# Holding each load back until the third last one has landed, in a fused SSM-convolution and MLP kernel

## The chip, the cores and the metric

The kernel runs on one core of a Trainium2 chip. The core has a tensor engine (PE, with its weight loads shown apart as PEld), a vector engine (DVE), a scalar engine (ACT), GpSimd (POOL) and a sync engine (SP) that issues most transfers. The transfers themselves are carried by 16 DMA engines. The metric is the device time of one execution in microseconds; lower is better.

## The reference

A block of sequence length S = 2048 and width D = 640. First a long convolution with a gate (H3 style), then an MLP with the Mish activation, both with a LayerNorm ahead and a residual sum behind:

```python
x = A_q
h = x + A_ref(layernorm(x), A_k, A_v, A_shift_k, A_ssm_k, A_ssm_D)
h2 = h + B_ref(layernorm(h), B_w1, B_b1, B_w2)

def A_ref(q, k, v, shift_k, ssm_k, ssm_D):
    k_shift = sum over t of k[s - 3 + t] * shift_k[:, 3 - t]     # 4 taps along the sequence
    kv = k_shift * v
    y = irfft(rfft(kv, 2S) * rfft(ssm_k, 2S))[:S]                # causal convolution, per channel
    return q * (y + kv * ssm_D)

def B_ref(x, w1, b1, w2):                                         # F = 1728
    a = x @ w1 + b1
    return (a * tanh(softplus(a))) @ w2
```

The sum over t is written here in short; the reference pads and adds four shifted copies. All inputs and the output are bf16.

## The kernel before

The convolution is done as a transform in matrix products. Stage s1 multiplies by a 128-point table (`cst`), stage s2 by a twiddle table G (128 matrices of 128 x 128), for the filter `ssm_k` (names s1k, s2k) and for the data kv (s1v, s2v). The two spectra are multiplied on DVE and POOL (p1, p2, with pair-swapped copies made by transfers, sw), and stages i1 and i2 go back. The MLP follows in five units of 256 or 512 rows: m1 (x @ w1), Mish on ACT (hb), m2 (@ w2), residual on DVE, output.

What the program does is cut into about a thousand named steps. A step is an object with a function that emits its instructions. The list `ORDER` (lines 26 to 96) gives every step with its engine (t = PE, a = ACT, v = DVE, p = POOL, d = a transfer issued by SP, s = one issued by ACT). `_schedule` (line 175) walks that list, gives each step an estimated start and assigns buffers in turn; the steps are then sorted by that start (line 932) and emitted one after the other (lines 933 to 938). Each engine carries out its own instructions in the order of emission. The framework adds the semaphore waits that data dependencies need; transfers take eight semaphores in turn, and a transfer waits until the earlier holder of its semaphore has landed.

The loads from HBM at the head of the kernel, all issued by SP:

- d_n0 to d_n4 (line 523), 512 KB each: the filter, into `rn`. Steps k1pe transpose it on PE (line 625) and k1ev copies it out of PSUM, shuffled (lines 419 and 421), into five places `kk_s`; two of these places lie over the loads n0 and n1 in `rn`.
- d_k0 to d_k3 (line 510), 640 KB each: k, into `ra`; transposed by ktpe (line 571). kv is later written over them in `ra` (line 600).
- d_v0, d_v1 (line 520), 1280 KB each: v, into `rb`, used when kv is formed (line 600). d_v0 also waits for PE, since its place holds a shuffled filter before.
- d_g0 to d_g7 (line 526), 512 KB each: table G, used by s2 (line 652 for the filter, 685 for the data).
- d_x0 (line 754), 640 KB: the first quarter of q, into `x0`, read first by the LayerNorm statistics on DVE (lines 776 and 777).

ACT issues three small transfers at the start (`cst`, `sk_r`, and the row `A_ssm_D`). In time the 20 loads come out of the sort in the order n2, n0, n3, n1, n4, k3, k2, x0, k1, g4, k0, g5, v1, g6, g0, g7, g1, v0, g3, g2.

Line 168 holds the planner's picture of PE's program being loaded in blocks while it runs: the first point at PE instruction 204, then one every 253, with two assumed durations:

```python
_MARK, _BLOCK, _FETCH, _SLOW = 204, 253, 2.2, 6.6
```

## Time and profile before

| | us |
|---|---|
| median of three runs (223.5 to 224.49) | 224.07 |
| the profiled execution | 224.86 |
| its span, from the first to the last instruction | 223.1 |
| first 5.7 us: PE busy 4.18, DMA at 217 GB/s | 5.70 |
| 43.7 to 90 us (products of the spectra, way back): PE busy 44.66 | 46.30 |
| 90 to 223 us (the MLP): PE busy 129.82, DMA at 36 GB/s | 133.00 |

The granted clock of TensorE is 1.0 throughout. The page divides the span into 40 slices of 5.6 us; one digit is the busy share in tenths:

```profile
PE   7998899999999999999999999999999999999994
...
DVE  0699989999999998999788898974400000004023
ACT  2689989999999999888870446800053454330000
POOL 1271950005596007235767714320000000000000
PEclk9999999999999999999999999999999999999999
DMA  6999991075999999100001401043350000000024
```

The first seven digits of the DMA row are the loads named above; the next block (slices 9 to 16) is the pair-swapped copies and the MLP's weights; what comes after is transposes and output. PE stands at 9 nearly throughout, but its matmuls are pipelined, and in the first 45 us it works hand in hand with DVE and ACT, which empty PSUM.

### The profile page before, as it was taken

The page shows a single profiled execution, that of the slowest core. Times are in us where ns is not written, and L with a number is a line of the kernel's source. Part 1 is how long each engine was busy: PE and PEld are TensorE (multiplying, and loading weights), DVE is VectorE, ACT ScalarE, POOL GpSimd, SP SyncE. Part 2 cuts the span into 40 slices and gives each one's busy share as a digit, 9 for nine tenths or more (in the row PEclk, how much of TensorE's full clock was granted, in tenths as well). Part 3 has the DMA queues.
Part 4 walks back from the last instruction along what each step waited for, and adds up shares of the span by engine and source line. Part 5 has one row for each costly group of instructions (what it writes and reads, how often), then busy time and mean ns, then how long its engine had stood idle before and what let it go on. Part 6 is the DMA issues. An engine that isn't in the chain of part 4 may idle for free.

```text
span 223.1 us, 6218 instructions
## 1 busy us (share of the span) xinstructions
PE 214.7 (96%) x2598; PEld 162.1 (73%) x2598; DVE 146.2 (66%) x317; ACT 134.4 (60%) x268; POOL 65.7 (29%) x106
## 2 busy tenths in 40 slices
PE   7998899999999999999999999999999999999994
PEld 2988899999877999988887644576645445675773
DVE  0699989999999998999788898974400000004023
ACT  2689989999999999888870446800053454330000
POOL 1271950005596007235767714320000000000000
PEclk9999999999999999999999999999999999999999
DMA  6999991075999999100001401043350000000024
GB/s 214 388 408 424 408 413 69 3 203 193 277 290 283 319 351 347 62 3 0 3 0 32 88 0 31 0 91 60 88 179 0 1 0 3 0 0 0 32 82 153
DMA packets 27342, 30.68 MB, mean 138 GB/s; under 512 B 9393, under 2 KB 23730, under 8 KB 26930
## 3 DMA queue, kind: packets, MB, share of 16 engines
q1 hardware_dynamic: 26880, 30.10, 41.1%
q8 instruction: 20, 0.33, 0.6%
q10 hardware_dynamic: 338, 0.18, 0.3%
q14 instruction: 8, 0.07, 0.1%
q0 software_dynamic: 96, 0.00, 0.0%
HBM read 20.45 MB, written 2.62 MB: 103 GB/s over the span
## 4 chain that ended last, share of the span: by engine, by line
PE 64%; DVE 13%; DMA 7%; ACT 7%; POOL 5%; issue 2%; SPq 0%; DVEq 0%; ACTq 0%; POOLq 0%
PE ps L915 21%; PE ps L898 19%; ACT uv L419 6%; DMA x<-in_A_q_dram 5%; PE ps L743 4%; PE ps L744 4%; PE ps L652 3%; PE ps L543 2%; PE ps L571 2%; DMA rn<-in_A_ssm_k_dram 2%; DVE st L776 2%; DVE st L822 2%; PE ps L595 2%; POOL r L782 2%; PE ps L916 2%
## 5 line engine op out<-in xcount | busy, mean ns | idle before, releaser
L915 PE MATMUL ps<-rn,uv 128*128 128x320 bf16 (+2 forms) x416 | 61.1, 299 | 0.2 <-DVE x L921 0.2
L903 ACT ACTIVATE uv<-ps,b1s 128x512 bf16<-128x512 f32 (+1 forms) x65 | 35.4, 610 | 39.1 <-PE ps L898 38.5
L898 PE MATMUL ps<-G 128*128 128x512 bf16 (+1 forms) x325 | 58.6, 337 | 0.0
L915 PEld LDWEIGHTS <-uv 128*128 128x128 bf16 x416 | 40.2, 98 | 17.5 <-issue 0.4
L419 ACT CAST uk<-ps 128x512 bf16<-128x512 f32 (+1 forms) x96 | 48.7, 702 | 2.6 <-PE ps L544 1.6
L898 PEld LDWEIGHTS <-G 128*128 128x128 bf16 x325 | 31.2, 98 | 23.9 <-issue 1.1
L921 DVE TENSOR_TENSOR xb<-ps,xb 128x320 bf16<-128x320 f32 (+2 forms) x12 | 5.7, 487 | 36.3 <-PE ps L916 35.8
L419 ACT CAST uv<-ps 128x512 bf16<-128x512 f32 (+2 forms) x57 | 28.7, 845 | 0.0
L921 DVE TENSOR_TENSOR xa<-ps,xa 128x320 bf16<-128x320 f32 x12 | 5.9, 488 | 21.6 <-PE ps L916 21.6
L827 POOL TENSOR_TENSOR r<-ve,mhalf 128x1 f32<-128x1 f32 x16 | 10.0, 630 | 32.7 <-DVE ve L824 32.7
L743 PE MATMUL ps<-a,uv 128*128 128x128 bf16 x160 | 18.8, 219 | 0.2
L421 DVE CAST uk<-ps 128x512 bf16<-128x512 f32 (+1 forms) x27 | 17.2, 669 | 1.4 <-PE ps L744 0.9
L743 PEld LDWEIGHTS <-uv 128*128 128x128 bf16 x160 | 17.9, 113 | 0.0
L421 DVE CAST uv<-ps 128x512 bf16<-128x512 f32 (+1 forms) x25 | 15.3, 677 | 0.0
L685 PE MATMUL ps<-uv,G 128*128 128x64 bf16 (+1 forms) x256 | 12.8, 197 | 0.8
L685 PEld LDWEIGHTS <-G 128*128 128x128 bf16 x256 | 11.1, 96 | 3.1 <-issue 2.1
L600 DVE TENSOR_TENSOR ra<-ps,rb 128x512 bf16<-128x512 f32 x20 | 12.5, 684 | 0.3 <-PE ps L596 0.3
L419 ACT CAST rb<-ps 128x512 bf16<-128x512 f32 (+1 forms) x28 | 10.6, 495 | 2.7 <-PE ps L803 2.7
L652 PE MATMUL ps<-uk,G 128*128 128x160 bf16 x128 | 12.1, 230 | 0.0
L782 POOL TENSOR_TENSOR r<-ve,mhalf 128x1 f32<-128x1 f32 x16 | 10.8, 672 | 1.3
L706 DVE TENSOR_TENSOR uv<-uv,uk 128x2048 bf16<-128x2048 bf16 (+1 forms) x11 | 10.9, 1022 | 0.0
L544 PE MATMUL ps<-cst,ra 128*64 128x128 bf16 x160 | 10.6, 220 | 0.1
(116 smaller groups left out, 376.7 us busy)
## 6 DMA issues: line engine op xcount, KB each, us to landing
G<-tab_g SPq DMA_DIRECT2D x8, 512.0 KB, 12.9
rn<-in_A_ssm_k_dram SPq DMA_DIRECT2D x5, 512.0 KB, 6.2
ra<-in_A_k_dram SPq DMA_DIRECT2D x4, 640.0 KB, 9.9
rb<-in_A_v_dram SPq DMA_DIRECT2D x2, 1280.0 KB, 13.1
G<-in_B_w_dram SPq DMA_DIRECT2D x5, 432.0 KB, 6.4
rn<-in_B_w_dram SPq DMA_DIRECT2D x1, 2080.0 KB, 9.8
rn<-uk SPq DMA_DIRECT2D x4, 512.0 KB, 5.1
rb<-uk SPq DMA_DIRECT2D x8, 256.0 KB, 7.9
```

The costliest lines, as they stand in the source:

```text
L419: nc.scalar.copy(o, i)
L421: nc.vector.tensor_copy(o, i)
L600: nc.vector.tensor_tensor(kv_w[:, m, :, 8 * h:8 * h + 8, l0:l0 + n], ps.rearrange("p (l t d) -> p d t l", l=n, t=8), raw_v[:, 8 * h:8 * h ...
L652: nc.tensor.matmul(ps[:, o:o + 160], g_v[:, f, :], KA[:, :, f, :], start=True, stop=True)
L685: nc.tensor.matmul(ps[:, fl * n:fl * n + n], g_v[:, f0 + h * kf + fl, :], VX[x][:, :, f0 + h * kf + fl, :], start=True, stop=True)
L706: eng.tensor_tensor(v, v, K[c.i][:, :, f0:f1, :], ALU.mult)
L743: nc.tensor.matmul(pz[:, k, :], V[c.i][:, dg // 4, :, dg % 4], a12[:, 0, :], start=True, stop=False)
L782: nc.gpsimd.tensor_tensor(r1[:, t2:t2 + 1], ve1[:, t2:t2 + 1], mhalf[:, 0:1], ALU.pow)
L898: nc.tensor.matmul(ph[:, 0:w], w1[:, dc, fc * P:fc * P + P], lnhT_of(u)[:, dc, 0:w], start=(dc == 0), stop=(dc == NDC - 1))
L903: nc.scalar.activation(hb_of(u)[:, fc, 0:w], rt.tile[:, 0:w], ACT.Mish, bias=b1s[:, fc:fc + 1], scale=1.0)
L915: nc.tensor.matmul(po[:, 0:d1 - d0], hb_of(u)[:, fc, tl * P:(tl + 1) * P], w2[:, fc, d0:d1], start=(fc == 0), stop=False)
L921: nc.vector.tensor_tensor(x, rt.tile[:, 0:d1 - d0], x, ALU.add)
```

## The change

A tile `step` of one partition and 32 elements is added. Of the loads, those whose names match `d_n`, `d_k`, `d_v`, `d_g` and `d_x0` are listed in the order of emission. Ahead of each of them from the fourth on, SP issues a transfer of one element, from the first element of the load three places earlier to an own element of `step`. That transfer waits for the earlier load to have landed, and SP, which works in order, issues nothing behind it until then. These are 17 transfers. The loads, their order among each other, and every step on the other engines stay.

```diff
+    step = cpool.tile([1, 32], BF16, name="step")
...
     order.sort(key=lambda o: (o.start, seq[id(o)]))
+
+    ends = {"d_n": lambda b: raw_n[b][0:1, 0:1], "d_k": lambda h: raw_k[0:1, 4 * h * D:4 * h * D + 1], "d_v": lambda h: rb[0:1, h * half:h * half + 1],
+            "d_g": lambda i: gt[0:1, 2048 * i:2048 * i + 1], "d_x": lambda h: (x0, xa, xb)[h][0:1, 0:1]}
+    loads = [o for o in order if o.eng == "dma" and re.match(r"d_([nkvg]\d|x0)$", o.name)]
+    after = {loads[i].name: loads[i - 3].name for i in range(3, len(loads))}
     with tc.manual_schedule():
         for o in order:
+            if o.name in after:
+                i = [l.name for l in loads].index(o.name)
+                w = after[o.name]
+                nc.sync.dma_start(step[0:1, i:i + 1], ends[w[:3]](int(w[3:])))
```

## The prediction

> **What bounds the kernel now.** I read the page first, then busy time by stage, the chain of waits, and the queue of SP, where the change sits.

> ```profile
> span 223.1 us, 6218 instructions
> ...
> PE 214.7 (96%) x2598; PEld 162.1 (73%) x2598; DVE 146.2 (66%) x317; ACT 134.4 (60%) x268; POOL 65.7 (29%) x106
> ```
> ```profile
> 5.70:17.20 11.50, 10.99 (x245) 10.41 (x247) 9.07 (x18) 8.71 (x14) 5.85 (x6) 1.00 1.01 400
> 17.20:27.80 10.60, 9.20 (x233) 8.70 (x227) 10.45 (x22) 10.15 (x21) 6.52 (x8) 1.00 1.02 414
> 27.80:43.70 15.90, 15.90 (x281) 15.64 (x283) 15.13 (x27) 15.09 (x33) 3.37 (x7) 1.00 0.43 173
> ```

> Columns of the stages: length, busy us of PE, PEld, DVE, ACT and POOL with counts, granted clock, share of the DMA engines, GB/s. The change touches the first 43.7 us alone. There the transfers run at 400 to 414 GB/s until all loads are in, while PE, DVE and ACT are nearly full too, at full clock. After 43.7 us nothing in the program is different, so a shift arises before that or not at all.

> ```profile
> 0.72 4.94 DMA rn<-in_A_ssm_k_dram
> 5.68 0.34 SPq L510
> 6.06 11.13 DMA x<-in_A_q_dram
> 17.22 0.90 DVE st L776 x2
> ...
> 24.55 2.38 PE ps L571 x36
> 26.93 0.83 issue
> 27.77 0.47 PE ps L571 x4
> ```
> ```profile
> 17.22 0.89 DVE L776 BATCH_NORM_STATS2 st<-x 128x6 f32<-128x320 bf16 x2 [0.64 <-DMA x<-in_A_q_dram]
> ```

> These are the chain that ended last (start, us, what) and one row of DVE's timeline. Two places count: DVE stands 0.64 us until load d_x0 lands, and PE stands 0.83 us at 26.93 us with nothing to wait for but its own instructions.

> ```profile
> 0.72 3.50 SPq L523 DMA_DIRECT2D rn<-in_A_ssm_k_dram  x5
> 4.26 1.75 SPq L510 DMA_DIRECT2D ra<-in_A_k_dram  x2
> 6.06 0.47 SPq L754 DMA_DIRECT2D x<-in_A_q_dram  x1
> ...
> 10.84 0.33 SPq L520 DMA_DIRECT2D rb<-in_A_v_dram  x1
> ```
> ```profile
> xb<-in_A_q_dram SPq DMA_DIRECT2D x1, 960.0 KB, 5.0
> ```

> SP issues five loads back to back and has ten out by 7.1 us. It already waits: eight semaphores are shared in turn, so a load goes out once the transfer eight before it has landed. The landing records of the trace give the last arrival of each load: n2 5.67, n0 6.92, n3 8.29, n1 9.58, n4 10.83, k3 12.68, k2 15.61, x0 17.19, k1 18.77, g4 20.05, k0 21.63, g5 22.89, v1 26.01, g6 27.28, g0 28.55, g7 29.81, g1 31.08, v0 34.28, g3 35.44, g2 36.68. They arrive in order, 1.25 us apart for 512 KB, 1.57 for 640 KB, 3.1 for 1280 KB. Each load is spread over 16 engines; the fastest finish 1.4 us (n2) to 2.7 us (v0) before the last.

> First uses, from the instructions that wait on these semaphores, give the slack: x0 0.0 (used at 17.22), n1 0.3 (9.89), n4 0.6 (11.40), k2 0.6 (16.22); every load from k1 on 2.6 us (g0, used at 31.16) or more (v1 3.0, k0 3.4, g7 3.6, v0 3.7, g3 3.7).

> **The change, part by part.** (1) 17 one-element copies are added on SP, one ahead of each load from the fourth on. The nearest issue rows take 0.33 us (L520 above), so 17 x 0.33 = 5.6 us of SP. SP's next work after the loads is at 43.70, and the last load would go out near 31.5: hidden. Queued behind a waiting copy are only later loads. PE, DVE, ACT and POOL keep their instructions and order.

> (2) The loads start later. A load is issued 0.02 us (seen wake, k0's issue at 8.31 after n3's landing at 8.29) + 0.33 us after the third last has landed. What it then needs beyond its bytes: d_x2 into xb, issued into an idle queue at 50.40, took 5.0 us for 960 KB, of which 960/512 x 1.25 = 2.34 are bytes, so 2.67 are fixed. So landing(i) = the later of landing(i-1) + its bytes and landing(i-3) + 0.35 + 2.67 + its bytes. Three 512 KB loads take 4.27 us instead of 3.75; for 640 KB the two loads still in flight (3.14 us) cover the 3.02. In numbers: n1 5.67 + 3.02 + 1.25 = 9.94 (+0.36), n4 11.19 (+0.36), k3 12.88 (+0.20), k2 14.53, and with the 1.35 us by which it came late before (15.61 - 12.68 - 1.57, while a piece of program was loaded on one engine) 15.88 (+0.27), x0 17.45 (+0.26). On the path: x0 +0.26 us, n1 0.05 past its slack. The later loads slip by at most 0.9 (g7 30.67, g2 37.5), inside 2.6.
> Bounds: below, 0, since the last engine never runs dry if the 0.97 us from issue to first packet (51.37 - 50.40) is all that counts: the new load is ready 0.35 + 0.97 = 1.32 us after the landing, and that engine still holds two loads, 2.5 us, less the 0.36 from its last packet to the landing (n0: 6.56 to 6.92). A gain is possible too: if another engine trails, x0 is earlier, worth at most DVE's 0.64. Above: n2 took 4.94 us for 512 KB, 3.67 fixed. Then n1 lands 10.94, n4 12.19, k2 16.53, x0 18.10 (+0.9), or 19.45 (+2.3) with the 1.35 on top. I take +0.3, nearest d_x2, an ordinary load with no small ones beside it.
> [...] This trace has 2.67, for a load from HBM issued by SP.

> (3) New holds. The copies read rn where ACT (L419, 10.15) and DVE (L421, 13.49) later overwrite loads n0 and n1 with shuffled filters, and in the built kernel these two wait for the copies. Nearest row: the 1.2 KB load of A_ssm_D on ACT's queue, on one engine beside the first loads, issued 1.61, landed 4.76: 3.15 us. Copy of n0: 6.94 + 3.15 = 10.09, just before 10.15; copy of n1: 9.60 + 3.15 = 12.75, before 13.49. Taken 0; above, the b1b loads of POOL took 5.3 to 5.6 us: 12.5 against 10.15 is 2.4, less the 0.5 us that ACT idles before 12.16, +1.9. A gain is excluded.

> (4) Instruction loading. The packet records show PE's program coming in 16 KB pieces on queue q8, on one engine each. Counted with the kernel's own 204 + 253n (line 168), PE passes the points at 10.51, 15.85, 21.74, 27.78, 35.05, 42.75, and pieces start 2.27, 3.42, 3.43, 3.67, then 0.36 and 0.53 us later: late while loads run, prompt when they don't. The third ends at 26.20, PE goes on at 27.77: the 0.83 us of "issue". With three loads in flight a piece waits for less: at 21.74 a fast engine would hold v1 until about 24.5, 2.8 us instead of 3.4, leaving 0.2 of the 0.83; the last engine holds 3.9, no gain. Ends 0 and -0.83 (a loss is excluded: fewer transfers stand ahead); I take -0.35.

> Sum: +0.3 + 0 - 0.35 = 0 (-0.05). The profiled execution took 224.86, 1.76 of it outside the span; it is 0.8 above the median 224.07, to which I apply the sum: 224.0. 0.5% (1.1 us) is about what a measurement of this kernel can tell from no change.

> **Rivals.**
> A, forecast (0.42): landings and instruction loading shift by less than 1.1 us together. For it: arrivals stay paced by the last engine, and 16 of 20 loads have slack of 0.6 us or more. 224.0, own range 223.0 to 225.1.
> B (0.25), slower: the queue runs dry. Mechanism: the loads' fixed time under load is that of n2 (3.67), not of d_x2; x0 lands +0.9 to +2.3, DVE and the chain follow one to one. It decides from a fixed time of about 3.5. For it: first packets take 0.3 to 1.4 us against 0.29 later in d_x2's own records. Against: n2 had three small loads of ACT beside it. 225.6.
> C (0.11), slower: the holds of (3); it decides once a copy takes over 3.2 us to land, by up to +1.9. For it: a copy stands behind two loads on its engine. Against: both writers come late. 225.4.
> D (0.22), faster: instruction loading turns prompt: -0.83, and x0 lands earlier, up to -0.64: -1.47, 222.6. For it: PE's wait on the chain, and the fetch at 52.01, which started 2.75 us later, when the single d_x2 was nearly through: it seems to wait for what is queued. Against: v1 stands there at just that point.
> [...]
> That the change does not hold the loads is excluded: the copies stand ahead of the loads in SP's own order.

> **How the numbers follow.** Faster by over 0.5% is D, 0.22; slower is B and C, 0.36; A is 0.42. The range has to reach both sides: 222.5 (D with 0.1 to spare) to 226.0 (B short of its +2.3), leaving out 0.1 each side at most.

> **What would show it.** SP's timeline with one load at a time from 5.7 us on, d_x0 issued near 11.2 instead of 6.06; landings within 0.5 us of those above (A), or x0 past 18 and GB/s below 370 between 5.7 and 27.8 (B); ACT L419 rn or DVE L421 rn waiting on DMA (C); the "issue" at 26.93 gone and pieces starting within 1 us (D). The forecast is wrong if the span up to 43.7 us changes by more than 1.1 us, or if anything after it does.

## The result, and the profile after

| | before | after |
|---|---|---|
| median, us | 224.18 | 232.01 (230.86 to 233.99) |
| ratio | | 1.0363, 95% interval 1.0284 to 1.0442 |
| profiled execution / its span, us | 224.86 / 223.1 | 232.57 / 230.8 |
| SP's first pair-swap transfer is issued at, us | 43.70 | 50.88 |

The kernel is slower by 7.8 us, outside the range. Of the 7.7 us by which the span grew, 7.2 have arisen when SP issues its first pair-swap transfer, which waits for the filter's spectrum; what follows adds 0.5. So the loss lies in the stage of the loads. One execution of c_free below (228.82 us) and two of cols6 (229.08 and 230.09) were longer than the others of the same kernel at a lower granted clock (0.992, 0.992 and 0.993 against 0.998 or more); the ratios leave these out, the medians count them.

Top of the page of the kernel after:

```profile
span 230.8 us, 6247 instructions
...
PE 217.8 (94%) x2598; PEld 164.8 (71%) x2598; DVE 147.0 (64%) x317; ACT 134.9 (58%) x268; POOL 65.6 (28%) x106
...
PEclk9979999979999999999999999999999999999999
DMA  6888979607599999910001121015242000000024
```

The loads now fill eight slices of the DMA row, where before six and a little of a seventh were enough, and two slices (the third and the ninth) have a lower granted clock. Busy time by stage, with the columns of the prediction:

```profile
5.70:17.20 11.50, 9.01 (x159) 8.36 (x159) 7.34 (x15) 6.20 (x8) 4.68 (x6) 0.90 0.85 286
17.20:27.80 10.60, 10.60 (x288) 10.19 (x285) 9.92 (x22) 9.94 (x21) 5.12 (x7) 0.95 0.92 295
27.80:43.70 15.90, 13.35 (x219) 12.86 (x217) 14.26 (x25) 14.28 (x28) 5.93 (x9) 1.00 0.89 324
```

The transfers fell from 400 and 414 to 286 and 295 GB/s, and the DMA engines' share from 1.01 and 1.02 to 0.85 and 0.92: they stand idle for part of the time in which all work waits for loads. PE's matmuls in the first of these stages fell from 245 to 159. The chain of waits up to 52 us (start, us, what):

```profile
0.72 4.46 DMA rn<-in_A_ssm_k_dram
5.20 0.76 SPq L944
6.00 4.27 DMA rn<-in_A_ssm_k_dram
10.29 0.63 SPq L944
10.97 5.79 DMA ra<-in_A_k_dram
16.82 0.58 SPq L944
17.44 5.72 DMA G<-tab_g
23.23 0.57 SPq L944
23.84 8.49 DMA rb<-in_A_v_dram
32.35 0.58 SPq L944
32.97 4.00 DMA G<-tab_g
37.03 0.57 SPq L944
37.65 7.34 DMA G<-tab_g
45.04 0.59 PE ps L653 x6
```

No work of a compute engine is in it before 45 us. It is load n2, copy, n1, copy, k2, copy, g4, copy, v1, copy, g7, copy, g3, and then PE. Before, the chain left the loads at 17.22 us and went through DVE and PE. SP's timeline and the waits of the same kernel (of a wait: us in total, times, longest):

```profile
5.20 0.76 SPq L944 DMA_DIRECT2D step<-rn  x1
6.00 0.58 SPq L524 DMA_DIRECT2D rn<-in_A_ssm_k_dram  x1
...
14.41 0.39 SPq L755 DMA_DIRECT2D x<-in_A_q_dram  x1
```
```profile
PEld L653 <- DMA G<-tab_g: 3.6, 2, 2.3
PEld L626 <- DMA rn<-in_A_ssm_k_dram: 3.3, 3, 1.9
...
DVE st L777 <- DMA x<-in_A_q_dram: 0.5, 1, 0.5
ACT rn L420 <- DMA step<-rn: 0.4, 1, 0.4
```

A copy takes SP 0.57 to 0.76 us. Of the waits for loads the two large ones are PE's: for n4 (1.9 us) and for g3 (2.3 us). DVE's wait for x0, which the prediction watched, is 0.5.

The links of the chain, from the landing records: time from one load's last arrival to the last arrival of the load it releases, less the bytes at the paces of before (1.25, 1.57, 3.1 us; for g3 those of v0 ahead of it too). What is left is not a fixed time alone: it also holds bytes of the loads in between, so it is not nothing before either, where no load waited for the one three places earlier. The forecast column holds the landings of the prediction's recurrence, with its 1.35 at k2 and, for g3, its 37.5 of g2 less 1.25. The fourth column is the first experiment below.

| link | before | forecast | third last by plain wait | after |
|---|---|---|---|---|
| n2 to n1 | 2.67 | 3.02 | 3.73 | 3.84 |
| n1 to k2 | 4.46 | 4.37 | 4.05 | 4.91 |
| k2 to g4 | 3.19 | 3.14 | 4.21 | 5.16 |
| g4 to v1 | 2.87 | 3.02 | 5.77 | 6.06 |
| v1 to g7 | 2.55 | 3.02 | 2.60 | 3.39 |
| g7 to g3 | 1.28 | 1.25 | 3.28 | 3.67 |
| sum | 17.0 | 17.8 | 23.6 | 27.0 |
| g3 has landed | 35.44 | 36.3 | 41.49 | 45.00 |

The sums are firmer than the single links: two other traces with the change (after_2 and after_warm below) give 27.5 and 26.9, but 4.48 and 5.90 for g4 to v1.

Before, g3 landed at 35.44 and was used 3.7 us later. After, it is 9.56 later; 9.56 less 3.7 of slack is 5.9, and the stretch from g3's use to the first swap grew from 4.56 (39.14 to 43.70) to 5.84: 1.3 more, together 7.2.

### The profile page after: what moved, and what is told of

Read it like the earlier page. It is cut to its first block, busy times and chain, and to the rows that moved or that the text cites. A ratio compares the mean times of both kernels' runs of the same rounds, so it can differ in the third digit from the quotient of the medians.

```text
span 230.8 us, 6247 instructions
## 1 busy us (share of the span) xinstructions
PE 217.8 (94%) x2598; PEld 164.8 (71%) x2598; DVE 147.0 (64%) x317; ACT 134.9 (58%) x268; POOL 65.6 (28%) x106
## 4 chain that ended last, share of the span: by engine, by line
PE 56%; DMA 17%; DVE 9%; ACT 8%; POOL 5%; issue 2%; SPq 2%; DVEq 0%; ACTq 0%; POOLq 0%
PE ps L916 21%; PE ps L899 18%; ACT uv L420 8%; DMA G<-tab_g 7%; DMA rn<-in_A_ssm_k_dram 4%; PE ps L744 4%; DMA rb<-in_A_v_dram 4%; PE ps L745 4%; DMA ra<-in_A_k_dram 3%; PE ps L544 2%; DVE st L823 2%; DVE st L777 2%; POOL r L783 2%; SPq L944 2%; PE ps L653 2%
## 5 line engine op out<-in xcount | busy, mean ns | idle before, releaser
L420 ACT CAST uk<-ps 128x512 bf16<-128x512 f32 (+1 forms) x96 | 48.7, 679 | 5.7 <-PE ps L653 3.1
L899 PEld LDWEIGHTS <-G 128*128 128x128 bf16 x325 | 31.2, 98 | 23.9 <-issue 1.1
L922 DVE TENSOR_TENSOR xb<-ps,xb 128x320 bf16<-128x320 f32 (+2 forms) x12 | 5.7, 488 | 36.3 <-PE ps L917 35.8
L420 ACT CAST uv<-ps 128x512 bf16<-128x512 f32 (+2 forms) x57 | 28.4, 762 | 0.0
L601 DVE TENSOR_TENSOR ra<-ps,rb 128x512 bf16<-128x512 f32 x20 | 13.2, 686 | 4.7 <-PE ps L597 4.6
L653 PE MATMUL ps<-uk,G 128*128 128x160 bf16 x128 | 12.6, 235 | 3.2 <-DMA G<-tab_g 3.2
L686 PEld LDWEIGHTS <-G 128*128 128x128 bf16 x256 | 11.0, 96 | 3.0 <-issue 1.9
L420 ACT CAST rb<-ps 128x512 bf16<-128x512 f32 (+1 forms) x28 | 10.6, 497 | 2.7 <-PE ps L804 2.7
L653 PEld LDWEIGHTS <-G 128*128 128x128 bf16 x128 | 9.2, 99 | 3.7 <-DMA G<-tab_g 3.6
L711 POOL TENSOR_TENSOR rn<-rn,uv 128x2048 bf16<-128x2048 bf16 x1 | 4.1, 4065 | 26.1 <-ACT uv L420 26.1
```

Source lines behind the costliest of these rows:

```text
L420: nc.scalar.copy(o, i)
L601: nc.vector.tensor_tensor(kv_w[:, m, :, 8 * h:8 * h + 8, l0:l0 + n], ps.rearrange("p (l t d) -> p d t l", l=n, t=8), raw_v[:, 8 * h:8 * h ...
L653: nc.tensor.matmul(ps[:, o:o + 160], g_v[:, f, :], KA[:, :, f, :], start=True, stop=True)
L686: nc.tensor.matmul(ps[:, fl * n:fl * n + n], g_v[:, f0 + h * kf + fl, :], VX[x][:, :, f0 + h * kf + fl, :], start=True, stop=True)
L899: nc.tensor.matmul(ph[:, 0:w], w1[:, dc, fc * P:fc * P + P], lnhT_of(u)[:, dc, 0:w], start=(dc == 0), stop=(dc == NDC - 1))
L922: nc.vector.tensor_tensor(x, rt.tile[:, 0:d1 - d0], x, ALU.add)
```

## The experiments

All ratios are to the kernel before on the same chip, with a 95% interval.

| run | median, us | ratio | interval |
|---|---|---|---|
| w3: third last load, plain wait | 227.12 | 1.0142 | 1.0090 to 1.0193 |
| w4: fourth last, plain wait | 224.47 | 1.0000 | 0.9975 to 1.0024 |
| w6: sixth last, plain wait | 224.32 | 0.9989 | 0.9968 to 1.0010 |
| w2: second last, plain wait | 238.15 | 1.0624 | 1.0574 to 1.0674 |
| c_free: copies that wait for no load | 225.14 | 1.0025 | 1.0009 to 1.0042 |
| w3_behind: w3, a copy behind each held load | 228.52 | 1.0175 | 1.0140 to 1.0210 |
| c4: the change, with the fourth last load | 225.75 | 1.0037 | 1.0013 to 1.0062 |
| after_2: the changed kernel again | 231.26 | 1.0281 | 1.0236 to 1.0327 |
| after_warm: the change, matmuls in PE's idle places | 231.87 | 1.0336 | 1.0290 to 1.0381 |
| w3_early: w3 for n1 to x0 only | 225.42 | 1.0050 | 1.0020 to 1.0080 |
| w3_late: w3 from k1 on only | 225.58 | 1.0060 | 1.0041 to 1.0079 |
| halves6: halves of 64 partitions, sixth last half | 242.93 | 1.0790 | 1.0741 to 1.0839 |
| halves_free: the same halves, no hold | 243.65 | 1.0841 | 1.0790 to 1.0892 |
| cols6: halves of the columns, sixth last half | 227.59 | 1.0104 | 1.0068 to 1.0141 |
| cols_free: the same column halves, no hold | 227.15 | 1.0128 | 1.0096 to 1.0161 |

**How many loads in flight.** The change does two things: it holds loads, and it puts copies on SP. The first group holds loads without copies. A semaphore wait is put on the load itself:

```diff
+    loads = [o for o in order if o.eng == "dma" and re.match(r"d_([nkvg]\d|x0)$", o.name)]
+    issued = []
     with tc.manual_schedule():
...
+            if o in loads:
+                issued.append(nc.cur_bb.bb.instructions[-1])
+                if len(issued) > 3:
+                    tc.add_manual_dep(issued[-1], issued[-1 - 3].name, mybir.DependencyInfo(mybir.DependencyClass.Sync, mybir.DependencyReason.DATA), reason="hold")
```

The others have 4, 6 or 2 in place of 3:

```diff
-                if len(issued) > 3:
-                    tc.add_manual_dep(issued[-1], issued[-1 - 3].name, ...
+                if len(issued) > 4:
+                    tc.add_manual_dep(issued[-1], issued[-1 - 4].name, ...
```

> The same hold, three loads in flight, but as a wait of the load itself on the third last load: the 17 one-element copies are gone. Theory 1 (depth: with three loads in flight the 16 engines run dry at every link, since the next load goes out only when the last of the 16 has finished): most of the loss stays, 229 to 231 us, GB/s between 5.7 and 45 us near 300 to 340; what is saved is the issue time of a copy, 0.58 us at each of the six links of the chain, 3.5 us at most. Theory 2 (the copies themselves delay the loads behind them on SP and on the one engine that carries them): the loss goes away, 224 to 225.5 us.

> As the hold by a plain wait without copies, but four loads in flight. Theory 1: the fourth load, 1.25 us of bytes or more, covers most of what was dry, 224.5 to 226.5 us. Theory 2: no copies, so 224 to 225 us, the same as with three in flight.

> Six loads in flight, plain wait, no copies. Both theories: nothing runs dry, 224 us within 0.5%. If it is still slower by 1% or more, a wait on a load's landing costs something that is not depth.

> Plain wait, two loads in flight. With three, the 19 loads after the first took 37.7 us (5.08 to 42.74) where their bytes alone take 29.1, so a load needed about 4.4 us beyond its bytes from the landing that releases it to its own landing, stragglers among the 16 engines included. Theory 1 with that figure: with two in flight 4.4 - 1.5 = 2.9 us are lost for every two loads, the last lands near 61 us and the time is 244 to 252 us. With the 2.7 us of an undisturbed load (the prediction's figure) only 1.2 us are lost for every two, the last lands near 45 us and the time is 228 to 232 us.

Third last: 227.12. On that chip the kernel before took 224.46, so the hold alone costs 2.7 us or 1.4%, and the changed kernel (after_2) took 231.26, 4.1 us more than the hold alone. The time lies between the ranges of the two theories: the hold costs by itself, and the copies cost more than the 3.5 us that the first one allowed them. The first two stages, and the chain, which is made of the same loads, without the copies:

```profile
5.70:17.20 11.50, 10.90 (x249) 10.17 (x248) 9.24 (x18) 8.76 (x14) 5.86 (x6) 1.00 0.93 321
17.20:27.80 10.60, 8.94 (x222) 8.44 (x217) 9.72 (x21) 9.33 (x19) 5.79 (x7) 1.00 0.95 336
```
```profile
0.72 4.36 DMA rn<-in_A_ssm_k_dram
5.10 4.97 DMA rn<-in_A_ssm_k_dram
10.08 5.60 DMA ra<-in_A_k_dram
15.70 5.44 DMA G<-tab_g
21.16 8.85 DMA rb<-in_A_v_dram
30.03 3.83 DMA G<-tab_g
33.87 7.61 DMA G<-tab_g
41.53 0.59 PE ps L652 x6
```

Fourth and sixth last: no change that could be measured. The stages of the kernel with the fourth last:

```profile
5.70:17.20 11.50, 10.94 (x239) 10.32 (x241) 9.07 (x18) 8.53 (x13) 5.86 (x6) 1.00 0.99 385
17.20:27.80 10.60, 10.07 (x246) 9.57 (x243) 10.41 (x22) 10.26 (x21) 6.47 (x8) 1.00 0.99 373
27.80:43.70 15.90, 15.90 (x298) 15.64 (x298) 15.71 (x28) 15.81 (x34) 3.44 (x7) 1.00 0.58 213
```

A tenth of the rate is gone here too (373 against 414 in the second stage, g2 landing at 39.80 in place of 36.68), but it lies within the slack of the late loads, and the time stays. So with four loads in flight the queue nearly holds out (DMA share 0.99 in both stages), and with three it doesn't (0.93 and 0.95).

Second last: 238.15, g2 landing at 53.76. Here four loads of 512 KB go out when the queue is nearly empty: the one other load in flight has landed 1.2 to 1.6 us after their issue. From issue to landing, 512 KB, from the issue and landing records:

| load, second last | issued | landed | us | less 1.25 of bytes |
|---|---|---|---|---|
| n3 | 5.21 | 9.02 | 3.81 | 2.56 |
| g4 | 22.20 | 25.53 | 3.33 | 2.08 |
| g0 | 36.31 | 39.79 | 3.48 | 2.23 |
| g2 | 50.38 | 53.76 | 3.38 | 2.13 |

So the fixed time of a nearly undisturbed load is 2.1 to 2.6 us, a little less than the 2.67 that the prediction took from d_x2. The other loads of 512 and 640 KB took 4.3 to 5.7 us from issue to landing, and 6.3 and 7.2 behind the two of 1280 KB. The arrivals of one load at its 16 engines lie 0.3 to 0.5 us apart for the four loads of the table and 1.0 to 3.6 us apart for the later others. The time lies between what the two theories gave for this run: the fixed time is neither that of an idle queue nor a constant 4.4.

**The copies.** Two kernels have the copies and take away what they do:

```diff
-                nc.sync.dma_start(step[0:1, i:i + 1], ends[w[:3]](int(w[3:])))
+                nc.sync.dma_start(step[0:1, i:i + 1], cst[0:1, 0:1])
```

> The 17 one-element copies stay where they are but read a table that is there from 2.9 us on, so they wait for no load. As copies and loads share eight semaphores in turn, four loads can be in flight. Theory 1: like four loads in flight without copies, plus little, 225 to 227 us. Theory 2: the loss stays with the copies, 229 to 232 us.

225.14: seventeen copies that wait for no load cost 0.25% (0.09 to 0.42). They take the eight semaphores in turn as well, so that four loads are in flight: n1 landed at 9.75, and x0, the fourth load behind it, went out at 9.77. That the changed kernel needs SP's time for the copies is not its cost; that the copy lies between a landing and the next issue can be. The next kernel has the holds of the plain wait and puts each copy behind its load:

```diff
+                if len(issued) > 3:
+                    tc.add_manual_dep(issued[-1], issued[-1 - 3].name, mybir.DependencyInfo(mybir.DependencyClass.Sync, mybir.DependencyReason.DATA), reason="hold")
+                    nc.sync.dma_start(step[0:1, len(issued):len(issued) + 1], cst[0:1, 0:1])
```

> Three in flight by a plain wait, and the 17 one-element copies (of a table that is there) each issued right behind a held load, where SP would idle. Theory 1a (the copy costs what it delays the load behind it, 0.6 us per link): 227 us as without copies. Theory 1b (the copy costs by its packet and completion on the one engine that carries it): 229 to 232 us, as in the changed kernel.

228.52, a ratio of 1.0175 against 1.0142 without copies. The two intervals overlap (1.0140 to 1.0210 and 1.0090 to 1.0193), so a cost of the copies behind the loads can't be told from none by the times. The trace shows none on the chain: the six links sum to 23.8 us, against 23.6 without copies. What the copies cost in the changed kernel they therefore cost by their place ahead of the load. From a landing to the issue of the load that it releases 0.64 to 0.82 us pass there in each of the six links, 4.2 in all, and 0.02 in the plain wait; 3.4 of the 4.2 are seen in the sum of the links (27.0 - 23.6).

With the fourth last load the copies cost little:

```diff
-    after = {loads[i].name: loads[i - 3].name for i in range(3, len(loads))}
+    after = {loads[i].name: loads[i - 4].name for i in range(4, len(loads))}
```

> The change with the fourth last load in place of the third last; the one-element copies stay. Theory (a load is released only when all 16 engines have landed one, and the fixed part of such a link is about 4.4 us, 5.0 with the 0.58 us copy): three loads' bytes between release and need take 3 x 1.53 = 4.6 us on average, so a link is short by about 0.4 us, five such links to g2, part of it in slack: 224.5 to 226.5, a ratio of 1.002 to 1.010, loads g3 and g2 landing at 38 to 42 us. Rival (the copies themselves cost, in SP's time or in the queue, however many loads are in flight): as far over the fourth last load by plain wait (224.47) as the changed kernel is over the third last by plain wait (227.1), that is 229 to 230.

225.75, 0.37% over the kernel before, as the theory of the links had it, and far from the 229 to 230 of its rival. One number of the change, the 3, decides over most of the loss.

> The changed kernel once more, on the same chip as the three others, so that they are compared with it directly: 231 to 233.5, ratio 1.03 to 1.043, if the loss is a steady one. If a part of it belonged to the first chip or to its clock there, under 230.

The same file as the change, on the chip of the plain wait: 231.26, with an interval (1.0236 to 1.0327) that overlaps that of the first runs, though the ratio is a little under the 1.03 expected. The loss is steady.

**Where along the loads.** The hold of the plain wait for a part of the loads:

```diff
-                if len(issued) > 3:
+                if len(issued) > 3 and len(issued) <= 8:
```
```diff
-                if len(issued) > 3:
+                if len(issued) > 3 and len(issued) > 8:
```

> The third last load by plain wait, but only for the fourth to the eighth load (n1 to x0); from the ninth on every load is free. With the hold only from the ninth load on the time was 225.58 (+1.4), with it from the fourth on 227.12 (+2.9). If the two halves of the delay simply add, this gives +1.5, 225.3 to 226. If the late loads' slack takes up what the early ones lost, because without a hold the queue catches up, only what x0 loses (0.7 us) is left: 224.4 to 225.1. No change (224.0 to 224.4) would say that the early links cost nothing by themselves and matter only as the start of the later ones.

> Three in flight by a plain wait, but only from the ninth load (k1) on; the first eight, to x0, go out as before. The prediction saw the early loads as the only ones on the path and 2.6 us or more of slack behind: then 224 to 224.5 us. Theory 1 (the loss adds up over the later loads until the slack is gone): 225.5 to 227 us.

With the hold from k1 on only, g3 landed at 39.98, 4.5 later than before and so past its slack of 3.7, and the first swap was at 44.46 (before 43.70): the late loads, which the prediction had within their slack, cost by themselves. Early part alone 1.0050, late part alone 1.0060, together 1.0110 against 1.0142 (1.0090 to 1.0193) for both: they add, within what can be told. With the hold on n1 to x0 only, x0 landed at 17.91 (before 17.19), g2 at 38.94, and the first swap was at 43.56, not later than before. That profiled execution was the fastest of a wide spread (224.74 to 228.09), so where the slower ones lose their time was not seen.

**The clock.** In two stretches of the first 50 us of the kernel after, the granted clock was half. The first two of these lines are the 3.41 us ahead of each, the third is the first of the two stretches itself (columns as in the stages):

```profile
11.43:14.84 3.41, 1.62 (x26) 1.49 (x24) 1.66 (x3) 0.32 (x2) 0.95 (x3) 1.00 0.93 353
42.15:45.56 3.41, 1.33 (x22) 1.13 (x20) 1.80 (x4) 1.46 (x4) 0.00 (x0) 1.00 0.57 221
14.84:18.25 3.41, 3.41 (x66) 3.30 (x65) 2.23 (x4) 2.24 (x4) 2.36 (x2) 0.50 0.78 234
```

PE was busy 1.62 and 1.33 of 3.41 us, because of the waits for n4 (its weight loads idle for 1.92 us) and g3 (2.28), and then the clock was 0.50 for 3.41 us (the second time from 45.56 to 48.97). The experiment fills the two waits with 13 matmuls whose results are overwritten:

```diff
+            if h and id(n) == id(raw_n[4]):
+                for _ in range(6):
+                    nc.tensor.matmul(ps[:, 0:512], wz[:, 0:P], wz[:, P:D], start=True, stop=True)
...
+            if h and f0 == 60:
+                for _ in range(7):
+                    nc.tensor.matmul(ps[:, 0:512], wz[:, 0:P], wz[:, P:D], start=True, stop=True)
```

> The changed kernel, with 6 and 7 matmuls on zeros (0.22 us each) put in at the two places where PE stood idle for 1.9 and 2.3 us for a load; they write a bank that the next step overwrites, the result is the same. Theory: the halves of the clock at 14.8 and 45.6 us come from this idleness; the clock is then 1.0, the time from the landing of load g3 to SP's first swap issue falls from 5.8 to about 4.5 us, the total by 1 to 1.7 us to 230 to 231. Rival: the clock does not depend on it or costs nothing, 231.5 to 232.5 us.

The clock stayed at 1.0 in the profiled execution, and from g3's landing (44.92) to the first swap (49.41) it took 4.49 us, against 5.88 (45.00 to 50.88) with the halved clock. The same stretch took 4.48 to 4.49 us in four other traces with the clock at 1.0 there (after_2, w3, w3_behind, w3_late). But the median, 231.87, can't be told from 232.01: a cost of 1.4 us was seen in that stage of one execution and not in the time. Nor do the matmuls keep the clock up each time: in two of the four executions its mean was 0.985 and 0.990.

**The step of the hold.** Is it the whole load as the unit of release that costs? Each load is cut in two, and each half held on the sixth last half, so that the bytes in flight are those of three loads. One line of each cut (the same for k, v, n and x0):

```diff
+    def part(ins):
+        issued.append(ins.ins)
+        if len(issued) > 6:
+            tc.add_manual_dep(issued[-1], issued[-7].name, ...)
...
-        return lambda: nc.sync.dma_start(gt[:, i * 2048:(i + 1) * 2048], dram["g"][:, i * 2048:(i + 1) * 2048])
+        return lambda: [part(nc.sync.dma_start(gt[p:p + 64, i * 2048:(i + 1) * 2048], dram["g"][p:p + 64, i * 2048:(i + 1) * 2048])) for p in (0, 64)]
```

> Every load is cut in two halves of 64 partitions, and each half is held, by a plain wait and without copies, until the sixth last half has landed: the bytes in flight are those of three loads, the transfers in flight are six. Theory (what counts is the bytes that lie queued while the slowest of 16 engines finishes one transfer; the finer step gives back half a load's time per link): between the third last and the fourth last load by plain wait, 224.5 to 226.5. Rival 1 (what counts is how many transfers are in flight): as the sixth last load by plain wait, 224.0 to 224.6. Rival 2 (bytes in flight alone, the step of no use): 227 or more, as the third last load by plain wait.

242.93, far over each theory. The stages of that kernel:

```profile
5.70:17.20 11.50, 8.82 (x185) 8.23 (x186) 7.63 (x16) 6.27 (x9) 4.26 (x6) 1.00 1.04 251
17.20:27.80 10.60, 6.37 (x142) 5.77 (x137) 5.99 (x13) 6.56 (x13) 2.66 (x4) 0.92 1.02 245
```

The engines are busy all the time (1.04, 1.02) and move 251 and 245 GB/s: not too few loads in flight, but slow packets, 264 ns for 4 KB in the mean against 170 before and 185 with the plain wait on the third last load. Three more kernels tell the cut from the hold: the same halves without the hold, and halves by columns with and without it.

```diff
-        if len(issued) > 6:
-            tc.add_manual_dep(issued[-1], issued[-7].name, ...)
```
```diff
-        return lambda: [part(nc.sync.dma_start(gt[p:p + 64, i * 2048:(i + 1) * 2048], dram["g"][p:p + 64, i * 2048:(i + 1) * 2048])) for p in (0, 64)]
+        return lambda: [part(nc.sync.dma_start(gt[:, o:o + 1024], dram["g"][:, o:o + 1024])) for o in (i * 2048, i * 2048 + 1024)]
```

> The halves by partitions with no hold of their own (at most eight in flight). Theory (a transfer that reaches only 64 partitions is slow by itself: 264 ns a packet, 1.04 us for 256 KB): the packets stay at 240 to 280 ns, and the time at 239 to 244, as with the hold (242.9). Rival (it was the hold on the sixth last half): packets back at 160 to 190 ns and 224 to 226.

> The same column halves with no hold of their own; the semaphores that the compiler hands out in turn let at most eight halves, four loads, be in flight. Theory (cut loads cost nothing where four loads' bytes are in flight): 223.8 to 225. Rival (the cut itself costs, in packets or in SP's issues, 40 of them at 0.35 to 0.6 us): 225.5 or more; then what the run with the hold lost is to be read against this one.

> As the run with halves, but each load is cut by columns: both halves fill all 128 partitions, with half of each row. Six halves in flight, plain wait on the sixth last. In the halves by partitions a packet of 4 KB took 264 ns where the same packet took 170 to 185 ns before and in the run with the third last load by plain wait, so the grain of the hold was not tested there. Here a row of 2 KB should take some 84 ns (on the line through 512 bytes in 28 ns and 4 KB in 159 ns). Theory (the link from landing to landing costs 4.4 us whole, and the finer step gives back half a load's bytes, 0.7 us, per link): between the third last (227.1) and the fourth last load (224.5) by plain wait, 224.5 to 226.5. Rival (bytes in flight alone, no gain by grain): 226.8 to 228. Rival (twice as many transfers cost more by themselves): over 228.

Without the hold the halves by partitions take 243.65, with 264 ns a packet and 251 GB/s in the first stage against 400 before: the slowness belongs to the cut. Why a transfer to 64 partitions has slower packets no run here shows.

The cut by columns costs 2.8 us even without a hold (227.15); in its profiled execution 1.5 us of it are there by the first swap (45.20 against 43.70). A part of it is in the packets: one of 2 KB took 84 ns in the median, as expected, where half of one of 4 KB is 79.5 (159 before). The second halves of n1, n4 and x0 landed 0.87, 0.94 and 0.56 us later than the whole loads before, which had 0.3, 0.6 and 0.0 us of slack. The hold on top of it gives 227.59 (1.0104), not told apart from 227.15 (1.0128), which seems to say that a finer step saves the cost. But the one trace of it is of an execution of 229.08, above all those that its ratio rests on (225.51 to 227.64), so its landings can't be set against the others. The question is not settled by these runs.

No kernel tried is faster than the one before; the fourth and the sixth last load by plain wait equal it.

## Why the prediction was wrong, step by step

**What bounds the kernel.** Right in that the change touches the first 43.7 us alone (7.2 of 7.7 us arise there). The two places that the prediction watched, x0 and the program loading, were not the ones that decided: g3 was, at the end of a chain through v1 and g7, and these three had 3.7, 3.0 and 3.6 us of slack.

**Step (2), the failed one: "landing(i) = the later of landing(i-1) + its bytes and landing(i-3) + 0.35 + 2.67 + its bytes", with later loads slipping "by at most 0.9".** The form of the recurrence held, but its size did not: along the chain it gives links of 17.8 us where 27.0 were measured, and g3 came 8.7 us after the forecast (45.00 against 36.3). Of the 9.2 us in the links, 5.8 are there with the hold alone (23.6). The 2.67 itself was not wrong, a nearly undisturbed load has 2.1 to 2.6. But it was taken from a load alone in the queue and put to loads that share it with two others. There the landing that releases the next load is that of the slowest of 16 engines, up to 2.8 us behind the fastest in the kernel after (0.6 to 2.8), and the fast ones can run out of work meanwhile: the DMA share is 0.93 and 0.95 in the plain wait and 0.85 and 0.92 in the change, against 1.01 and 1.02 before. The share shows less than half of it, though. In the plain wait the rate fell by 20 and 19% (321 and 336 GB/s against 400 and 414), the share by 8 and 7%; the rest is in packets that take long. The median 4 KB packet takes 159 ns in every kernel with whole loads, but of those that started from 5.7 to 27.8 us 0.8% took over 300 ns before, 2.2% with four loads in flight, 5.4% with three, 8.2% in the change and 12.5% with two. Why a packet takes long is not shown. Before, a spread of 1.1 us (n4) to 2.8 us (v0) cost nothing; that the fast engines then go on to the next loads is argued, not shown engine by engine. Each load leaves 16 landing records, and what waits for it goes on behind the last of them: in the kernel after, those of g4 lie from 21.91 to 23.17, and the copy that waits for g4 was issued at 23.23. That each record is one engine's is read from their number. What makes an engine late, and whether it is the same one in each load, stays open: the records do not name the engine of a packet.

The other 3.4 us are step (1).

**Step (1), the copies: "17 x 0.33 = 5.6 us of SP ... hidden".** Wrong twice. One copy takes 0.57 to 0.76 us, nearer to the 0.61 of ACT's one-partition row A_ssm_D than to the 0.33 of a load over 128 partitions. And while SP's total is hidden (0.25% with copies that wait for nothing), a copy ahead of a held load is part of each link: landing, 0.57 to 0.76 us of copy, issue. The prediction did count 0.35 there, as the wait and issue of the copy, but no issue of the load on top, which it left to the 2.67. Why the issue of a one-element copy takes longer no run here isolates; the filter's loads over 128 partitions took 0.56 to 0.70 us of SP in the same kernel.

**The lower bound, "the last engine never runs dry".** This was an argument on one engine, the last one of before. It held where four loads were in flight (224.47), not with three.

**Rival B** named the right mechanism, a queue that runs dry (DMA share 0.85 and 0.92 against 1.01 and 1.02), and its threshold, a fixed time of 3.5 us and thus 3.85 with the 0.35 of issue, was passed: just so in the mean of the links with the plain wait (3.9), clearly in the change (4.5), where before and forecast have 2.8 and 3.0. It was priced at x0 only, +0.9 to +2.3, and x0 landed 2.56 later (19.75 against 17.19). But a shortfall per link adds up, and the late loads' slack of 2.6 to 3.7 us was used up by g3's 9.56. The step that was missing is the sum of the shortfall over all six links (9.2 us), against the slack of the last load.

**Step (3) and rival C.** Nearly right: of the holds, the wait of ACT at the shuffled filters (L420 rn on the copy) is 0.4 us, once; DVE's does not appear.

**Step (4) and rival D.** Not seen. In the kernel after, PE passes the loading points at 10.94, 19.19, 24.34, 30.20 and 38.75, and the pieces start at 11.75, 21.59, 27.69, 33.67 and 41.06, 0.8 to 3.5 us later. With three loads in flight a piece is still late. PE also still has an "issue" stop of 0.69 us, at 29.49 (before 0.83 us, at 26.93). With the fourth last load by plain wait the stop near 26.8 was absent (PE busy 10.07 us from 17.2 to 27.8, 9.20 before), and the time the same.

**What it would show.** "x0 past 18 and GB/s below 370" was the sign of B, and it appeared (19.75; 286 and 295).

## What to carry to other kernels

A load that waits for an earlier load to land makes a chain; price it link by link over all loads (measured with several in flight, not one alone), add whatever the issuing engine does between landing and issue, and set the sum against the slack of the last load, not of the first. Here four loads of 512 to 1280 KB in flight cost nothing that could be measured (1.0000, 0.9975 to 1.0024) and three cost 1.4% without and 2.8 to 3.6% with a one-element copy in each link. A hold on a landing seems to give back the lead that the faster of the DMA engines have; that is argued from the spread of the landings (0.6 to 2.8 us) and the DMA share (0.85 and 0.92 against 1.01 and 1.02).
